# FFT filter and two gated layers on one core: the first batch's FFT kept on chip, float64 weights joined in two VectorE steps, order of instructions left to the scheduler

## The chip, the core and the metric

The kernel runs on one core of a Trainium2 chip. The metric is the time of one execution in device microseconds (us). Five engines work side by side, each through its own queue in order: TensorE (PE, matmuls; its weight loads are listed as PEld), VectorE (DVE), ScalarE (ACT), GpSimd (POOL) and SyncE (SP, which here only issues transfers). ACT and POOL issue transfers too. A transfer runs on 16 DMA engines that all queues share. TensorE writes only to PSUM; DVE and ACT bring results from there to SBUF; POOL works in SBUF alone.

## The reference

```python
def _attn_ref(x, filt_r, filt_i):            # x: 8 x 3072 x 256
    X = np.fft.rfft(x, axis=1)
    Y = X * (filt_r + 1j * filt_i)[None]
    return np.fft.irfft(Y, n=x.shape[1], axis=1).astype(np.float32)

def _moe_ref(x, w_in, w_out, g_ln):          # per token: 256 -> 1024 -> 256
    h = x @ w_in
    e = np.exp(h - np.max(h, axis=-1, keepdims=True))
    solu = h * (e / (np.sum(e, axis=-1, keepdims=True) + 1e-09))
    mu, var = mean(solu), mean((solu - mu) ** 2)
    return ((solu - mu) / np.sqrt(var + 1e-06) * g_ln) @ w_out

def _moe2_ref(x, w1, w2, w3, w_out):         # 256 -> 768 -> 256
    return np.maximum(np.maximum(x @ w1, x @ w2), x @ w3) @ w_out
```

x and the filter are float32; the six weight matrices are float64.

## The kernel before

There are 8 batches of 3072 rows and 256 columns. Each batch goes through four FFT steps: a (a transform over 128 points), b (over 24 points, with the filter's products), c (24 points back) and d (128 points back). Behind d come the layers, in six tiles of 512 tokens for each batch: h (x @ w_in, four pieces of 128 tokens), z (@ w_out), m (the three maxout products, six pieces), o (the last product, two pairs). That makes 48 tiles; the main loop runs over them and, for each, through a string of tokens (`ORDER`, for the first tile `FIRST`), which names the pieces in the order in which they are written. FFT steps of the next batches lie between them (`slots`, s0 to s4). Batches 1 to 7 run in float16 pairs (high and low parts), three matmuls for one product.

Batch 0 comes first and alone: its four FFT steps run in float32 ahead of the main loop. `first_a` (L282) computes step a and writes it to DRAM (`scr_a0`). For each of eight groups u, `first_load_b` reads a piece of it back in another layout, `first_b` (L294) does step b, `products` (L229) the filter, `first_turn` (L310) turns the result with TensorE transposes, and `first_c` (L325) does step c and writes to DRAM (`scr_0`), from which `load_d` reads the tiles of step d. The tables of steps b and c come as 144 KB pieces for each u.

Between these steps the weights are prepared (`steps`, `fills`, `jobs`). A block of float64 is loaded as pairs of 32-bit words (`wload`), turned to float32 in `wprep` (ACT takes the high word as a float, L615, and POOL raises small values, L616) and `wconv` (three VectorE steps on integers, L628, L630, L632), 20 blocks in all. `colsum` (ACT, PE, DVE) bounds the size of each matrix, `wscale` makes a power of two of it, and `wsplit` (L669 to L676) writes the float16 pairs. `center_wo1` takes the column mean off w_out.

The whole program stands in `tc.manual_schedule()`: each engine gets its instructions in the order in which the code writes them. The `run` helper delays the late half of an item behind the next item's matmuls.

Of the kernel before, what the change touches and what calls it, by code (L numbers as in the profile page):

```python
# [9 lines left out]
I32 = mybir.dt.int32  # L10
BF16 = mybir.dt.bfloat16
# [16 lines left out]
def kernel(  # L28
# [47 lines left out]
    scr_a0 = drm.tile([128, 24, 256], F32, name="scr_a0")  # L76
# [6 lines left out]
    b_f, c_f = (  # L83
        t[:, 1].rearrange("p k h s -> p (k h s)").bitcast(F32).rearrange("p (u q s) -> u p q s", u=8, q=4)
        for t in (dft_b, dft_c)
    )
    dft_b, dft_c = dft_b[:, 0], dft_c[:, 0]
# [114 lines left out]
    spare = []  # L202

    def first_load_b(u):
        t = two.tile([96, 4, 256], F32, tag="bin", name="bin0")
        src = scr_a0.rearrange("k n d -> (k n) d").rearrange("(u q p) d -> u p q d", q=4, p=96)
        SP.dma_start(out=t, in_=src[u])
        bin_t[0, u] = t
# [6 lines left out]
    def first_load_c(u):  # L215
        if u % 2 == 0:
            t = two.tile([96, 768], F16, tag="ct", name="ct0", bufs=1)
        else:
            t = spare[0][:96]
        t = t.bitcast(F32).rearrange("p (q s) -> p q s", q=4)  # L220
        SP.dma_start(out=t, in_=c_f[u])
        ct_t[0, u] = t
# [6 lines left out]
    def products(pss, ft, u):  # L229
        yfs = []  # L230
        for dc in range(2):
# [10 lines left out]
            G.tensor_tensor(p1[:, :, 0, :], p1[:, :, 0, :], p2[:, :, 1, :], op=ALU.subtract)  # L242
            G.tensor_tensor(p1[:, :, 1, :], p1[:, :, 1, :], p2[:, :, 0, :], op=ALU.add)
            if u == 0:
                G.tensor_copy(p1[:, 0, :, 0], t)
            yfs.append(p1)
# [35 lines left out]
    def first_a(s):  # L282
        pss = []
        for h in range(2):
            ps = rtile("aps")
            c = s * 1024 + h * 512
            PE.matmul(ps, dA_f, x_t[0][:, c:c + 512], start=True, stop=True)
            pss.append(ps)
        ao = two.tile([128, 1024], F32, tag="ao" if s % 4 < 2 else "yt", name="ao0")
        S.activation(ao[:, 0:512], pss[0], AF.Copy)  # L290
        V.tensor_copy(ao[:, 512:1024], pss[1])
        SP.dma_start(out=scr_a0[:, 4 * s:4 * s + 4, :], in_=ao.rearrange("p (n d) -> p n d", n=4))

    def first_b(u):  # L294
# [11 lines left out]
        def out():  # L306
            yT_t[0, u] = products(pss, f_t.pop((0, u)), u)
# [16 lines left out]
    def first_c(u):  # L324
        yt, ct = yT_t.pop((0, u)), ct_t.pop((0, u))  # L325
        zf = two.tile([128, 1024], F32, tag="ao", name="zf")
        pss = []
        for i in range(2):
            ps = rtile("cps")
            for q in range(2):  # L330
                c = (2 * i + q) * 256
# [864 lines left out]
```

## Time and profile before

| | us |
|---|---|
| median of 3 runs | 2925.84 (2925.73 to 2934.33) |
| profiled execution, its own time | 2924.07 |
| its span, first to last instruction | 2922.3 |
| TensorE busy / idle in the span | 2804.4 / 117.9 |
| VectorE busy | 1987.1 |
| ScalarE busy | 1203.8 |
| GpSimd busy | 1154.4 |
| mean granted TensorE clock | 0.985 of 2.4 GHz |

The profile is one execution. Its span is 1.8 us shorter than its own time, and that is 1.8 us under the median. A busy TensorE is counted from modelled ends of pipelined matmuls, so "busy" there means that work is in its queue without a gap. The rows that matter come below.

### The profile page before, as it was taken

How to read it: one execution, taken by the hardware profiler on the slowest of the kernel's cores; microseconds unless marked ns; L12 is line 12 of the kernel's file. 1: busy time of each engine (PE TensorE's matmuls, PEld its weight loads, DVE VectorE, ACT ScalarE, POOL GpSimd, SP SyncE). 2: the span in 40 equal slices, each digit the busy share in tenths (PEclk: the TensorE clock that was granted, in tenths of full speed). 3: DMA queues.
4: the chain of work that ended last, by engine and by line, in shares of the span. 5: the costliest groups of instructions: out<-in, count | busy, mean ns of one | idle time of the engine just before them, and what ended most of it. 6: DMA issues, size and time to landing. Idle time of an engine off the chain costs nothing. (4 is left out here: it accounts for less than half of the span.)

```text
span 2922.3 us, 48692 instructions
## 1 busy us (share of the span) xinstructions
PE 2804.4 (96%) x18676; PEld 1545.9 (53%) x18676; DVE 1987.1 (68%) x3932; ACT 1203.8 (41%) x1988; POOL 1154.4 (40%) x1205
## 2 busy tenths in 40 slices
PE   6689999999999999999999999999999999999999
PEld 4444554455545555555555555555555555555555
DVE  6787676676767677767766777667677667656553
ACT  3454444343444344434444443444344443433332
POOL 4542562444334443344433443344433444333322
PEclk7899999999999999999999999999999999999999
DMA  8433795476545764458534774447654466322221
GB/s 293 128 98 94 181 201 110 124 152 135 119 111 124 144 157 98 115 126 175 125 93 120 147 171 90 136 112 150 142 121 110 102 145 144 82 63 60 55 62 29
DMA packets 726504, 361.07 MB, mean 124 GB/s; under 512 B 620992, under 2 KB 672064, under 8 KB 726272
## 3 DMA queue, kind: packets, MB, share of 16 engines
q1 hardware_dynamic: 697168, 250.96, 38.8%
q0 software_dynamic: 28960, 106.95, 13.8%
q8 instruction: 146, 2.39, 0.4%
q14 instruction: 86, 0.70, 0.1%
q10 hardware_dynamic: 144, 0.07, 0.0%
HBM read 130.32 MB, written 75.50 MB: 70 GB/s over the span
## 5 line engine op out<-in xcount | busy, mean ns | idle before, releaser
L483 POOL TENSOR_TENSOR ul<-u,uh 128x1024 f16<-128x1024 f32 x191 | 406.3, 2127 | 1085.5 <-issue 625.4
L542 PE MATMUL mps<-z,wm 128*128 128x512 f16 x1728 | 655.0, 379 | 25.0 <-DVE am L550 16.8
L543 PE MATMUL mps<-z,wm 128*128 128x512 f16 x1728 | 655.0, 379 | 0.0
L544 PE MATMUL mps<-z,wm 128*128 128x512 f16 x1728 | 654.8, 379 | 0.0
L550 DVE SCALAR_TENSOR_TENSOR am<-mps,am 128x512 f32<-128x512 f32 x576 | 396.7, 689 | 231.0 <-ACT am L548 162.2
L452 ACT ACTIVATE u<-hps,mx,scl 128x1024 f32<-128x1024 f32 (+1 forms) x195 | 232.2, 1191 | 417.7 <-DVE mx L449 410.8
L446 DVE TENSOR_REDUCE mx<-hps 128x1 f32<-128x1024 f32 (+1 forms) x195 | 234.4, 1203 | 204.7 <-PE hps L437 204.0
L554 POOL TENSOR_TENSOR h<-am,h 128x512 f16<-128x512 f32 x240 | 279.4, 1164 | 212.5 <-ACT h L553 212.3
L482 ACT ACTIVATE uh<-u 128x1024 f16<-128x1024 f32 x192 | 202.9, 1057 | 322.5 <-DVE u L463 322.4
L553 ACT ACTIVATE h<-am 128x512 f16<-128x512 f32 x288 | 181.3, 629 | 369.9 <-DVE am L550 369.9
L463 DVE SCALAR_TENSOR_TENSOR u<-hps,mx,u 128x1024 f32<-128x1024 f32 (+1 forms) x195 | 246.8, 1267 | 106.4 <-ACT u L452 89.2
L569 PE MATMUL ops<-wo,h 128*128 128x256 f16 x1152 | 314.7, 273 | 4.5 <-ACT o L575 4.5
L570 PE MATMUL ops<-wo,h 128*128 128x256 f16 x1152 | 314.8, 273 | 0.0
L571 PE MATMUL ops<-wo,h 128*128 128x256 f16 x1152 | 314.8, 273 | 0.0
L435 PE MATMUL hps<-win,y 128*128 128x512 f16 x768 | 293.3, 382 | 6.7 <-DVE u L463 6.7
L437 PE MATMUL hps<-win,y 128*128 128x512 f16 x768 | 293.6, 382 | 0.2 <-DVE y L411 0.2
L436 PE MATMUL hps<-win,y 128*128 128x512 f16 x768 | 293.4, 382 | 0.0
L543 PEld LDWEIGHTS <-wm 128*128 128x128 f16 x1728 | 169.1, 98 | 230.6 <-issue 38.6
L522 PE MATMUL zps<-ln,wo 128*128 128x512 f16 x752 | 287.1, 382 | 2.4 <-ACT o L575 2.4
L523 PE MATMUL zps<-ln,wo 128*128 128x512 f16 x752 | 287.1, 382 | 0.0
L544 PEld LDWEIGHTS <-wm 128*128 128x128 f16 x1728 | 169.1, 98 | 204.0 <-issue 0.3
L542 PEld LDWEIGHTS <-wm 128*128 128x128 f16 x1728 | 169.2, 98 | 198.7 <-ACT wst L671 0.3
(207 smaller groups left out, 4344.7 us busy)
## 6 DMA issues: line engine op xcount, KB each, us to landing
scr_a<-ao SPq DMA_DIRECT2D x48, 512.0 KB, 3.5
out_dram<-o SPq DMA_DIRECT2D x95, 256.0 KB, 2.3
xt<-in_x_dram POOLq DMA_DIRECT2D x42, 512.0 KB, 5.9
ft<-in_filt_dram POOLq DMA_DIRECT2D x56, 384.0 KB, 5.3
bin<-scr_a POOLq DMA_DIRECT2D x56, 384.0 KB, 5.2
scr_z<-zt SPq DMA_DIRECT2D x56, 384.0 KB, 3.6
din<-scr_z POOLq DMA_DIRECT2D x42, 512.0 KB, 5.3
bt<-in_dft_b_dram POOLq DMA_DIRECT2D x56, 144.0 KB, 4.1
```

The source lines that it names most:

```text
L435: PE.matmul(o, y[:, dc, 0, tk], win[:, 0, dc, w], start=(dc == 0), stop=False)
L436: PE.matmul(o, y[:, dc, 0, tk], win[:, 1, dc, w], start=False, stop=False)
L437: PE.matmul(o, y[:, dc, 1, tk], win[:, 0, dc, w], start=False, stop=(dc == 1))
L483: (V if (b, g, i) == (0, 0, 3) else G).tensor_tensor(ul, u, uh, op=ALU.subtract)
L522: PE.matmul(ps, wo1[:, 0, c, w], ln[:, 0, c], start=(c == 0), stop=False)
L542: PE.matmul(pss[k], wm[k][:, 0, dc, w], z[:, dc, 0], start=(dc == 0), stop=False)
L543: PE.matmul(pss[k], wm[k][:, 1, dc, w], z[:, dc, 0], start=False, stop=False)
L544: PE.matmul(pss[k], wm[k][:, 0, dc, w], z[:, dc, 1], start=False, stop=(dc == 1))
L550: V.scalar_tensor_tensor(am, ps, 2.0 ** -15, am, op0=ALU.mult, op1=ALU.max)
L569: PE.matmul(o, h2[:, j, 0, tk], wo2[:, 0, j], start=(j == 0), stop=False)
L570: PE.matmul(o, h2[:, j, 0, tk], wo2[:, 1, j], start=False, stop=False)
L571: PE.matmul(o, h2[:, j, 1, tk], wo2[:, 0, j], start=False, stop=(j == 5))
```

## The change

**On chip.** `scr_a0` and its round trip go. `first_a` now takes x as the stationary operand (48 matmuls of 128 columns in place of 12 of 512), so that its result stands with d on the partitions, and writes it to two SBUF tiles. `first_turn_a` turns each group with eight TensorE transposes and two ACT copies. `first_c` swaps its operands as well, its result goes to an SBUF tile `zx`, and `first_turn_z` turns it (eight transposes for each of six tiles). Only tiles 2 to 5 of step d still go through DRAM.

**Tables and filter.** Both float32 tables of a group u come in one transfer, all eight issued at the start, into the space of the later weights (`wm`, `wo2`). The filter is loaded into `win`, `wo1` and others. The filter's scale goes into step d (`ky`).

**Weights.** `wprep` computes a float32 on ACT with a factor, and POOL makes from the 16 bits in the middle of each float64 the low word that rounds right; `wconv` then needs two VectorE steps, both with two tensor inputs. w_out is prepared first, w_in next, w1 and w2 next in the second `ln` buffer, w3 in `yt` buffers, w_out2 last.

**Order.** `tc.manual_schedule()` goes, and the scheduler sets each engine's order. In the first tile h0 and h1 of the second tile move from ahead of the loop to `FIRST`.

On PE one round of batch 0's FFT was, before (eye_f is the identity, yps a transposed product, cps step c, bps step b):

```order
L332 MATMUL cps<-yt_429,ct_372 96x256 x4
L300 MATMUL bps<-bt_416,bin_418 128x96 x8
L316 MATMUL yps<-eye_f,p_516 96x128 x4
L316 MATMUL yps<-eye_f,p_522 96x128 x4
L332 MATMUL cps<-yt_505,f_115 96x256 x4
```

and is now, with the turning of step a (tps) in it:

```order
L336 MATMUL cps<-wm_77,yt_387 128x96 x8
L301 MATMUL bps<-wm_79,bi 128x96 x8
L321 MATMUL yps<-eye_f,yhl_90 96x128 x4
L321 MATMUL yps<-eye_f,yhl_91 96x128 x4
L287 MATMUL tps<-eye_f,a_104 96x128 x8
L336 MATMUL cps<-wm_78,yt_456 128x96 x8
```

A round grew by eight transposes, and step c is cut as step b is.

On ACT, around the first use of batch 0's step d (y is its float16 pair, which h needs; wab is the colsum's input), before:

```order
L321 ACTIVATE yt_726<-yps 96x1024
L337 ACTIVATE zf<-cps,pf 96x512 x2
L644 ACTIVATE wab<-wo_193 128x1024
L644 ACTIVATE wab<-wo_194 128x1024
L615 ACTIVATE wst<-wln 128x2x256 x2
L337 ACTIVATE zf<-cps,pf 96x512 x2
L675 ACTIVATE wo_76<-wo_193,pwo_791 128x1024
L675 ACTIVATE wo_76<-wo_194,pwo_791 128x1024
L410 ACTIVATE y<-dps,scl 128x512 x2
```

and now (zx is step c's result on chip, zps its transposes, din the input of step d):

```order
L341 ACTIVATE zx<-cps 128x24x16 x2
L707 ACTIVATE win<-win_125,pwin 128x1024
L707 ACTIVATE win<-win_126,pwin 128x1024
L362 ACTIVATE din_860<-zps_855 128x512
L643 ACTIVATE w_880<-wln 128x512
L643 ACTIVATE w_881<-wraw 128x256
L740 ACTIVATE wmean<-wmean 128x256
L676 ACTIVATE wab<-wo_123 128x1024
L676 ACTIVATE wab<-wo_124 128x1024
L362 ACTIVATE din_909<-zps_899 128x512
L436 ACTIVATE y<-dps,ky 128x512 x2
```

The split of w_out (wo_76) left the stretch ahead of y; its column mean (wmean) and the sizes behind it (wab) stand ahead of y now as then.

On DVE, in a late tile without FFT work, where h's second piece meets the first m pieces (u is h's product, am the maximum of the three m products, BN the statistics of u), before:

```order
L459 TENSOR_SCALAR mx<-st,scl 128x1
L463 SCALAR_TENSOR_TENSOR u<-hps,mx,u 128x1024
L550 SCALAR_TENSOR_TENSOR am<-mps,am 128x512 x6
L446 TENSOR_REDUCE mx<-hps 128x1
L449 TENSOR_SCALAR mx<-mx,scl 128x1
L467 BN_STATS mv<-u 128x6 x2
```

and now:

```order
L485 TENSOR_SCALAR mx<-st,scl 128x1
L489 SCALAR_TENSOR_TENSOR u<-hps,mx,u 128x1024
L576 SCALAR_TENSOR_TENSOR am<-mps,am 128x512
L493 BN_STATS mv<-u 128x6
L576 SCALAR_TENSOR_TENSOR am<-mps,am 128x512
L493 BN_STATS mv<-u 128x6
L494 BN_AGGR mv<-mv 128x2
L576 SCALAR_TENSOR_TENSOR am<-mps,am 128x512
L495 COPY st<-mv 128x1
L576 SCALAR_TENSOR_TENSOR am<-mps,am 128x512 x3
```

The statistics moved from behind the next piece's maximum, where ACT's exponential left DVE free, to between the am steps. On PE the sequence of pieces is the same from the second batch's step b on, to the end. POOL's queue now begins with five transfers of batch 1 (two table pieces, two filter pieces, one table c) and, behind the last matmul of `first_a`, the reload of dA.

The diff, cut:

```diff
+REBIAS = 2.0 ** -112
+TOP = (1 - 2.0 ** -8) * 2.0 ** -13
-FIRST = "s0 s1 h2 m0 x0 x1 m1 x0 m2 s2 x0 x0 x0 x0 x2 h3 m3 d m4 m5 g0 f o0 s3 o2 g1 s4"
+FIRST = "h0 m0 x0 h1 m1 x0 x0 h2 m2 x0 x0 x0 s0 s1 s2 x2 h3 m3 d m4 m5 g0 f o0 s3 o2 g1 s4"
...
+    bc_f = dft_b[:, 1:3].rearrange("p t k h s -> p (t k h s)").bitcast(F32).rearrange("p (u q s) -> u p q s", u=8, q=8)
...
     def first_load_tab(u):
-        t = two.tile([96, 4, 96], F32, tag="bt", name="bt0")
-        SP.dma_start(out=t, in_=b_f[u])
-        bt_t[0, u] = t
+        w = (wm + [wo2])[u // 2]
+        names = "h c n" if u < 6 else "h j n"
+        t = w[:96, u % 2].rearrange(f"p {names[2:]} -> p ({names[2:]})").bitcast(F32).rearrange("p (q s) -> p q s", q=8)
+        SP.dma_start(out=t, in_=bc_f[u])
+        bt_t[0, u], ct_t[0, u] = t[:, 0:4], t[:, 4:8]
...
     def first_a(s):
+        for dc in range(2):
+            ps = rtile("aps")
+            for n in range(4):
+                c = s * 1024 + n * 256 + dc * 128
+                PE.matmul(ps[:, n * 128:(n + 1) * 128], x_t[0][:, c:c + 128], dA_f, start=True, stop=True)
+            pv = ps.rearrange("p (n i m) -> p i m n", n=4, i=2)
+            S.activation(af[0][:, dc, :, 4 * s:4 * s + 4], pv[:, 0], AF.Copy)
+            V.tensor_copy(af[1][:, dc, :, 4 * s:4 * s + 4], pv[:, 1])
+
+    def first_turn_a(u):
+        av = af[u // 4].rearrange("p e (q m) n -> p e q (m n)", q=16)
+        bi = two.tile([128, 1024], F32, tag="ao", name="bi")
+        bin_t[0, u] = bi[:96].rearrange("p (q d) -> p q d", q=4)
         pss = []
-        for h in range(2):
-            ps = rtile("aps")
-            c = s * 1024 + h * 512
-            PE.matmul(ps, dA_f, x_t[0][:, c:c + 512], start=True, stop=True)
+        for i in range(2):
+            ps = rtile("tps")
+            for q in range(2):
+                for dc in range(2):
+                    c = q * 256 + dc * 128
+                    PE.transpose(ps[:96, c:c + 128], av[:, dc, 4 * (u % 4) + 2 * i + q], eye_f)
             pss.append(ps)
-        SP.dma_start(out=scr_a0[:, 4 * s:4 * s + 4, :], in_=ao.rearrange("p (n d) -> p n d", n=4))
+
+        def out():
+            for i in range(2):
+                S.activation(bi[:96, i * 512:i * 512 + 512], pss[i][:96], AF.Copy)
+        return out
...
     def first_c(u):
-                PE.matmul(ps[:96, q * 256:q * 256 + 256], ct[:, 2 * i + q], yt[:96, c:c + 256], start=True, stop=True)
+                PE.matmul(ps[:, q * 96:(q + 1) * 96], yt[:96, c:c + 128], ct[:, q], start=True, stop=True)
...
+                S.activation(
+                    zx[0][:, :, dc, 16 * u:16 * u + 16],
+                    pss[dc][:, :384].rearrange("p (m n) -> p n m", n=24), AF.Copy,
+                )
...
+    def first_turn_z(g):
...
+                    PE.transpose(ps[:, c:c + 128], zx[0][:, 4 * g + 2 * i + n, dc], eye_f)
...
+        if g < 2:
+            din_t[0, g] = t
+        else:
+            SP.dma_start(out=scr_0[:, 4 * g:4 * g + 4, :], in_=t)
...
-            S.activation(dst, raw.bitcast(F32).rearrange("p a (n w) -> p a n w", w=2)[:, :, :, 1], AF.Abs)
-            G.tensor_scalar(dst, dst, LEAST, None, op0=ALU.max)
+            S.activation(dst, raw.bitcast(F32).rearrange("p a (n w) -> p a n w", w=2)[:, :, :, 1], AF.Copy, scale=REBIAS)
+            lo = raw.rearrange("p a (n w) -> p a n w", w=2)[:, :, :, 0]
+            top = raw.bitcast(U16).rearrange("p a (n w) -> p a n w", w=4)[:, :, :, 1]
+            G.tensor_scalar(lo, top, TOP, 7.5 * 2.0 ** -8 - 0.5, op0=ALU.mult, op1=ALU.add)
...
-            V.tensor_scalar(bits, bits, 3, 0x3FFFFFF8, op0=ALU.logical_shift_left, op1=ALU.bitwise_and)
+            V.scalar_tensor_tensor(lo, hi, -0x80000000, lo, op0=ALU.bitwise_and, op1=ALU.bitwise_or)
         for bits, lo, hi in wide:
-            V.scalar_tensor_tensor(bits, hi, -0x40000000, bits, op0=ALU.bitwise_and, op1=ALU.bitwise_or)
-        for bits, lo, hi in wide:
-            V.scalar_tensor_tensor(bits, lo, 29, bits, op0=ALU.logical_shift_right, op1=ALU.bitwise_or)
+            V.scalar_tensor_tensor(bits, bits, 3, lo, op0=ALU.logical_shift_left, op1=ALU.bitwise_or)
...
-    with tc.manual_schedule():
...
+    for i in range(11):
+        b_out = first_b(i - 1) if 0 < i < 9 else None
+        t_out = first_turn(i - 2) if 1 < i < 10 else None
+        a_out = first_turn_a(i) if i < 8 else None
...
+        c_out = first_c(i - 3) if i > 2 else None
...
+    first_turn_z(0)
+    cen[4]()
```

## Rows read from the trace of the kernel before

**Rows 1.** Busy time of each engine over the whole span, from the page.

```profile
PE 2804.4 (96%) x18676; PEld 1545.9 (53%) x18676; DVE 1987.1 (68%) x3932; ACT 1203.8 (41%) x1988; POOL 1154.4 (40%) x1205
```

**Rows 2.** Windows: stretch, PE, PEld, DVE, ACT, POOL busy us, TensorE clock, DMA share, GB/s.

```profile
15.00:20.00 5.00, 2.69 (x7) 0.90 (x5) 5.00 (x7) 1.19 (x2) 0.00 (x0) 1.00 1.03 420
```

**Rows 3.** Windows of the FFT, of the tile behind it, and of a late one.

```profile
50.00:100.00 50.00, 39.94 (x223) 32.19 (x223) 37.47 (x69) 27.96 (x42) 34.80 (x41) 0.89 0.61 179
100.00:150.00 50.00, 28.02 (x177) 16.79 (x176) 39.22 (x88) 23.35 (x36) 19.26 (x13) 0.76 0.34 106
...
2750.00:2800.00 50.00, 50.00 (x287) 26.88 (x285) 30.12 (x62) 18.29 (x31) 14.62 (x10) 1.00 0.26 59
```

**Rows 4.** TensorE's waits, 0 to 260 us: who for whom, us, times, longest.

```profile
PE bps L300 <- issue: 15.2, 1, 15.2
PE wps L652 <- ACT wab L644: 13.0, 5, 4.4
PE dps L396 <- DMA din<-scr: 8.6, 1, 8.6
PE yps L316 <- POOL p L243: 7.5, 7, 2.1
PE hps L435 <- DVE u L463: 6.7, 1, 6.7
```

**Rows 5.** TensorE's waits, 260 us to the end, the first and the third.

```profile
PE mps L542 <- DVE am L550: 14.9, 18, 1.1
...
PE ops L569 <- ACT o L575: 4.5, 3, 2.1
```

**Rows 6.** TensorE's timeline, start and us: batch 0's steps, the first h, the second tile's z.

```profile
4.90 12.79 PE L287 MATMUL aps<-xt,dA 128*128 128x512 f32 x24 [4.90 <-DMA xt<-in_x_dram]
32.89 7.11 PE L300 MATMUL bps<-bt,bin 96*128 96x96 f32 x32 [15.21 <-issue]
...
45.46 3.57 PE L300 MATMUL bps<-bt,bin 96*128 96x96 f32 x16
...
85.95 1.92 PE L300 MATMUL bps<-bt,bin 96*128 96x96 f32 x16
...
111.46 3.75 PE L396 MATMUL dps<-dD,din 128*128 128x128 f32 x16 [8.58 <-DMA din<-scr]
115.00 0.50 PE L435 MATMUL hps<-win,y 128*128 128x512 f16 x1
...
221.45 0.38 PE L522 MATMUL zps<-ln,wo 128*128 128x512 f16 x1
```

**Rows 7.** TensorE's timeline: transposes at either clock, the column mean, a later step d.

```profile
42.57 1.09 PE L316 MATMUL yps<-eye_f,p 128*96 128x128 f32 x4 [2.57 <-POOL p L245]
...
79.89 1.04 PE L316 MATMUL yps<-eye_f,p 128*96 128x128 f32 x8
...
82.50 3.62 PE L704 MATMUL wmean<-wo,ones 128*128 128x256 f32 x16
...
149.96 2.05 PE L396 MATMUL dps<-dD,din 128*128 128x128 f32 x16 [0.31 <-DVE u L463]
```

**Rows 8.** Groups of 0 to 221 us on DVE, POOL and ACT: count, busy, mean ns.

```profile
L616 POOL TENSOR_SCALAR wst<-wst 128x512 f32<-128x512 f32 x12 | 19.5, 1635 | 22.8 <-ACT wst L615 22.8
...
L242 POOL TENSOR_TENSOR p<-p,p 128x192 f32<-128x192 f32 x16 | 11.4, 710 | 7.7 <-DVE p L236 7.7
...
L337 ACT ACTIVATE zf<-cps,pf 96x512 f32<-96x512 f32 x16 | 10.5, 677 | 2.7 <-PE cps L332 2.4
...
L628 DVE TENSOR_SCALAR wst<-wst 128x512 int32<-128x512 int32 x12 | 9.6, 824 | 6.7 <-POOL wst L616 6.7
...
L321 ACT ACTIVATE yt<-yps 96x1024 f32<-96x1024 f32 x8 | 8.1, 1015 | 18.0 <-PE yps L316 18.0
...
L711 POOL TENSOR_TENSOR wo<-wo,wmean 128x256 f32<-128x256 f32 x8 | 6.6, 861 | 0.0
...
L630 DVE SCALAR_TENSOR_TENSOR wst<-wln,wst 128x512 int32<-128x512 int32 x6 | 5.7, 972 | 0.0
```

More of the change, by code (lines that the diff above doesn't have):

```diff
@@ L10 @@
 I32 = mybir.dt.int32
+U16 = mybir.dt.uint16
 BF16 = mybir.dt.bfloat16
@@ new lines @@
+    src = x[0].rearrange("(p r) d -> p (r d)", r=24)
+    x_t[0] = one.tile([128, 6144], F32, tag="x", name="xt")
+    for i in range(6):
+        SP.dma_start(out=x_t[0][:, i * 1024:(i + 1) * 1024], in_=src[:, i * 1024:(i + 1) * 1024])
+    S.dma_start(out=dA_f, in_=dft_a[:, 2:4].rearrange(flat).bitcast(F32))
+    G.dma_start(out=eye_sb, in_=eye)
+    load_filter()
+    V.memset(ones, 1.0)
+    V.memset(mhalf, -0.5)
+    V.memset(alpha_w, 1.0)
+    V.tensor_copy(eye_f, eye_sb)
+    ut = [two.tile([128, 1024], F32, tag="bin", name="wo32") for _ in range(2)]
@@ new lines @@
+    yt = [two.tile([128, 2, 2, 512], F16, tag="y", name="win32") for _ in range(2)]
+    wo1_32 = [wview(t, 4, 256) for t in ut]
+    win_32 = [wview(t.rearrange("p a b c -> p (a b c)").bitcast(F32), 1, 1024) for t in yt]
+    todo = [b for i in range(2) for b in blocks(w_out, wo1_32[i], 4 * i)]
+    todo += [(w_in[k * 128:(k + 1) * 128, c:c + 512], win_32[k][:, :, c:c + 512])
+             for k in range(2) for c in (0, 512)]
+    wm_32 = [wview(wln[1].bitcast(F32)[:, k * 1536:], 2, 768) for k in range(2)]
@@ new lines, in pre, with job, conv @@
+    def pre(i):
+        def job():
+            wprep(todo[i][1], got[i])
+        return job
+    def conv(*n):
+        return lambda: wconv([(todo[i][1], got.pop(i)) for i in n])
+    first_load_tab(0)
+    load_f(0)
+    for u in range(1, 8):
+        first_load_tab(u)
+        load_f(u)
+        if u < 6:
+            get(u - 1)()
+    G.dma_start(out=dD_f, in_=dft_d[:, 2:4].rearrange(flat).bitcast(F32))
+    G.dma_start(out=gsb, in_=g_ln.rearrange("(c p) -> p c", p=128))
+    for s in range(6):
+        first_a(s)
+        absmax(0, s)
@@ new lines, in split, with scale, job, pads @@
+    def split(dst, v, nm, eng=V):
+        return lambda: wsplit(dst, v, pw[nm], eng)
+    def scale(nm, c0, n):
+        def job():
+            pw[nm] = wscale(wmax[:, c0:], n, nm)
+        return job
+    def pads():
+        for t in yhl_t:
+            G.memset(t[:, :, 96:128], 0.0)
+    zx.append(one.tile([128, 6144], F32, tag="x", name="zx").rearrange("p (n e m) -> p n e m", n=24, e=2))
+    cso = colsum(wo1_32, 256, wmax, 2)
+    csw = colsum([v[:, :, :] for v in win_32], 1024, wmax, 0)
@@ new lines @@
+    h(0)
+    cso[0]()
+    for i in range(17, 19):
+        get(i)()
+    h(1)
+    cso[1]()
+    scale("o1", 2, 1)()
+    split(wo1[:, :, 0:4], wo1_32[0], "o1")()
+    split(wo1[:, :, 4:8], wo1_32[1], "o1")()
+    first_turn_z(2)
+    h(2)
+    pre(16)()
+    conv(16)()
+    for f in cs[0]:
+        f()
+    first_turn_z(3)
+    z_part(0)
+    cs[1][0]()
+    h(3)
+    cs[1][1]()
+    z_part(1)
+    for f in cs[2]:
+        f()
+    run(d_item(0, 1))
+    flush()
+    z_part(2)
+    scale("m", 4, 6)()
@@ new lines, in split_m @@
+    def split_m(k, c):
+        eng = (V, G, G)[k]
+        if k < 2:
+            split(wm[k][:, :, :, c:c + 384], wm_32[k][:, :, c:c + 384], "m", eng)()
+            return
+        for i in range(2):
+            split(wm[k][:, :, i:i + 1, c:c + 384], yts[i][:, :, c:c + 384], "m", eng)()
+    for k in (2, 1, 0):
+        split_m(k, 0)
+    z_part(3)
+    for k in (2, 1, 0):
+        split_m(k, 384)
+    first_turn_z(4)
+    first_turn_z(5)
+    get(19)()
+    wo2_32 = wview(one.tile([128, 6144], F32, tag="x", name="wst"), 6, 256)
```

475 lines of the change are left out of this document (210 added, 265 removed).

## The prediction

> **What bounds the kernel now.** I read the busy shares first. TensorE is busy 2804.4 us of a span of 2922.3 [rows 1], so 117.9 us are idle, and no other engine is above 68%. The windows show where the idle time lies: a late stretch of 50 us is busy for all 50 at the full clock of 2.4 GHz, while 50 to 100 us is busy 39.94 at a granted clock of 0.89 and 100 to 150 us only 28.02 at 0.76 [rows 3]. So the late tiles are bound by TensorE's own work, which the change leaves in number and order, and the start is bound by chains through other engines. TensorE's waits of the first 260 us name them: 15.2 us ahead of the first step b, 13.0 for the sizes of the weights, 8.6 for step d's input from DRAM, 7.5 for POOL's products, 6.7 for a DVE product [rows 4]. After 260 us the waits are many and small; the largest sum, 14.9 us, is in 18 pieces of 1.1 at most [rows 5].
>
> The timeline gives four marks: step a runs from 4.90 to 17.7, the first step b starts at 32.89, the first h at 115.00, and the second tile's z, from which on the order is nearly the same, at 221.45 [rows 6]. I sum the change between these marks, against the profiled execution's own 2924.07 us; the median of the runs lies 1.8 above it.
>
> **Step a to the first step b.** Now 12.79 us for step a, then 15.2 of waiting for the DRAM round trip [rows 4, 6]. After: 48 matmuls of 128x128 in float32. Eight of them (16 records) in step d took 2.05 us at full clock [rows 7], so 6 x 2.05 = 12.3 us, from 4.90 to 17.2. Then one copy out of PSUM, eight transposes and two more copies. The nearest copy is 0.677 [rows 8], eight transposes are 1.04 at full clock [rows 7]: 17.2 + 0.7 + 1.0 + 1.4 = 20.3. The five transfers of batch 1 that now stand at the head of POOL's queue are 1.23 MB; at the 420 GB/s that the engines moved in this stretch [rows 2] they can push the loads behind them back by 2.9 us, so 20.3 to 23.2. I take 22.5, near the upper end, since the first pass through each engine is included in it. Against 32.89 that is 10.4 us earlier. The removed writes and reads of `scr_a0` (6.3 MB) free more transfer time than the 1.23 MB take.
>
> **The eight rounds.** Now step b of the third group starts at 45.46 and that of the eighth at 85.95 [rows 6], 40.5 us for five rounds, 8.1 each. After, TensorE has in one round eight transposes of step a, eight matmuls of step b, eight transposes of the products and eight matmuls of step c, which now has step b's shape. At full clock 1.04 + 1.92 + 1.04 + 1.92 = 5.9 us; at half clock (3.57 for step b at 45.46, 1.09 for four transposes) 2.2 + 3.6 + 2.2 + 3.6 = 11.6 [rows 6, 7]. ACT: two new copies of 0.677, one of 1.015, two for step c at 0.677 at most [rows 8], so 3.7, and about 1.7 of weight work, 5.4. POOL: four product steps of 0.710 and 1.5 blocks of `wprep` at 1.635 [rows 8], 5.3. DVE was busy 37.47 of 50 there [rows 3], 6.1 of each 8.1; it loses a join step of 0.824 for each block [rows 8], 1.2 a round, and one of the two left writes with a stride. POOL's new form, with 16-bit strided input, is not in the trace: its floor is the old 1.635, and at twice that a round on POOL is 7.7. A round therefore costs between 5.9 (TensorE, all else hidden) and 8.1 (as now). I take 7.3, nearer to today's value, because the chain step b, DVE, POOL, transposes stays and is what TensorE waits for now, while the waits on loads go. The eighth step b then starts at 22.5 + 7 x 7.3 = 73.6.
>
> Here **a rule speaks against the change**. The trace shows the eight transposes at 79.89 in 1.04 us, 0.13 each, and step b six microseconds later at its fast 1.92 [rows 6, 7]: transposes did not keep the clock down there. The Trainium skill, "TensorE: Matmul & The Clock Gate", section "Part 4: PE-mode transpose", says that the full clock does not engage for a transpose and gives about 275 ns for one in a real kernel. By that the 112 added transposes would cost 31 us instead of 112 x 0.13 = 14.6, and more of the PE's rounds would run at half rate; the row decides for the smaller figure, and what the slower clock would give stands among the rivals.
>
> **From the last step b to the first h.** Step b 1.9, products on DVE and POOL about 4, transposes 1.0, copy 1.0, step c 1.9, two copies 1.4, transposes of `zx` 1.0: 73.6 + 12.2 = 85.8. No DRAM lies between; the 8.6 us of waiting [rows 4] is gone. But what is late next is the order on ACT: the pair y that h needs stands behind the column mean and both sizes (wab). The mean takes 3.62 on TensorE [rows 7], to 89.4; its copy 0.4; POOL takes it off in 8 steps of 0.861 [rows 8], 6.9, to 96.7; then one size, one copy and the first y, each near 0.7 to 1.0. h starts at about 99. Step d's own 2.05 is hidden beside POOL's 6.9. Against 115.00 that is 16 us earlier.
>
> **From h to the second tile's z.** Now 106.4 us, DVE busy 39.22 of the first 50 [rows 3]. Added: four turns of `zx` on TensorE (4.2 to 8.8), eight ACT copies at 0.677 (5.4), the scale and split of w_out, which were finished ahead of h before. Taken away: a join step in eight blocks on DVE, 8 x 0.824 = 6.6 if the two left cost no more than before (0.972 [rows 8]), and the 6.7 us [rows 4] in front of an h piece, since both h pieces of the second tile now lie between m pieces that TensorE can do meanwhile. Bounds: 8 us better (DVE's saving in full and part of the wait) to 10 worse (all turns and copies on the path). I take 0, as the added work is on the engines that have room and the removed on the one that is near its limit. The gain at 221.45 is 16 us.
>
> **The 47 tiles behind.** TensorE's sequence is the same. What moved is the order on DVE, ACT and POOL. On DVE the statistics of u now lie between the am steps. In a late tile that costs nothing: two pieces of m hold six PSUM buffers, so DVE is only late when it falls a whole m piece behind. In tiles with FFT work it can cost. On ACT the store's first copy now comes ahead of uh, which helps the waits on it (4.5 us at one line [rows 5]). Gain and loss have no row; the nearest are the waits that exist, 14.9 and 4.5 us, so at most some 20 us better, and, with one more wait of 0.8 (14.9 / 18) in each of some 36 tiles with FFT work, 29 worse. I take 0, the row of today.
>
> The sum: 2924.07 - 16 = 2908 for a profiled execution, **2910 us** for the median.
>
> **Rivals.** (1) The clock stays at 1.2 GHz through the rounds. For it: step b at 45.46 still took 3.57, against 1.92 at 85.95 [rows 6], and a round has more short transposes than now. Against: 0.89 on the mean from 50 to 100 us and the fast rows there [rows 3, 6]. A round is then 11.6 us on TensorE; the point from which the change loses is 7.3 + 16 / 7 = 9.6 us a round. At 11.6 the first h is at 129 instead of 99, 14 later than now, and the time is 2924 + 14 + 2 = 2940. By the section of the Trainium skill named above this would be the likely case; the rows speak against it. (2) The gain of 16 us is eaten behind h: turns, copies and the split of w_out all lie on the path (10 us), and POOL's new form is slow (another 3 to 6 in the rounds): 2920 to 2926, no change that can be told. (3) The new order opens a wait in each FFT tile, DVE in statistics or a product while TensorE needs an am step: 36 x 0.8 = 29 us, 2910 + 29 = 2939. For it: DVE and POOL share the work of these tiles in an order set without this chip's waits. Against: the tiles have two m pieces of slack. (4) The new order removes waits: 2910 less 10 to 20, 2890 to 2900.
>
> **How the numbers follow.** Forecast and its bounds of 2896 to 2917: 0.52. Rival 4: 0.13. Rival 2: 0.18. Rival 1: 0.09. Rival 3: 0.08. Within 0.3% is 8.8 us, about what a measurement of this kernel can tell from no change: faster means below 2917.1, slower above 2934.6. Faster: 0.52 + 0.13 = 0.65. Same: rival 2 and the milder halves of 1 and 3, 0.18 + 0.02 = 0.20. Slower: 0.15. The range of eight in ten reaches from 2890, the end of rival 4, to 2937, which takes in rival 2 and part of 1 and 3.
>
> **What would show it.** In the profile after: first step b near 22.5, rounds of 7.3, the first h near 99 and waiting for y behind the sizes, the second tile's z near 205; TensorE's idle time behind that point near 40 us as now. A first h after 107 makes the rounds wrong (look at the granted clock and at POOL's `wprep`); an h near 99 with z after 212 makes the middle wrong; z near 205 and a time over 2917 means the new order in the tiles costs.

## The result, and the profile after

The kernel after the change takes 2903.35 us (2896.60 to 2906.97, median of 4 runs). Its ratio to the kernel before is 0.990 (95% interval 0.9878 to 0.9922), some 29 us less (the two medians of this group of runs, 2928.59 for the kernel before, lie 25 apart). 2910 was forecast, with a range of 2890 to 2937. The profiled execution took 2904.83 us, 19.2 less than that of before, and its span is 2903.1. From one group of runs to the next the median of the kernel before lay between 2926.6 and 2936.1, so the experiments are compared by their ratio to it.

The busy time of the engines, from the page of the kernel after (before: [rows 1]):

```profile
PE 2804.4 (97%) x18923; PEld 1561.0 (54%) x18924; DVE 2048.4 (71%) x3918; ACT 1236.9 (43%) x2024; POOL 1139.9 (39%) x1208
```

Over the whole span TensorE is busy exactly as long as before, so by the sums the whole gain is idle time. It is not the same work, though. Up to the second tile's z (line of before, then of after, columns as in the windows below):

```profile
0.00:221.45 221.45, 155.07 (x870) 102.08 (x871) 162.41 (x314) 97.39 (x143) 106.27 (x106) 0.84 0.55 172
```

```profile
0.00:193.68 193.68, 156.75 (x1118) 116.96 (x1119) 150.35 (x310) 109.93 (x183) 92.75 (x117) 0.94 0.61 166
```

TensorE has 248 records more there, 112 of them transposes, and is busy hardly longer, at a mean granted clock of 0.94 instead of 0.84. The idle time up to that z fell from 66.4 to 36.9 us. So the higher clock has a part in the gain of the start: it paid for the added work. DVE is busy 61 us longer over the whole span, although it has 18 instructions of the join less; that comes back below. The windows of the start (stretch, busy us of PE, PEld, DVE, ACT, POOL, then TensorE's granted clock, DMA share, GB/s; before: [rows 3]):

```profile
0.00:50.00 50.00, 40.88 (x327) 39.32 (x328) 34.74 (x62) 24.50 (x48) 22.97 (x46) 1.00 0.99 298
50.00:100.00 50.00, 37.18 (x252) 30.64 (x252) 39.00 (x84) 31.84 (x53) 26.59 (x36) 0.90 0.27 86
100.00:150.00 50.00, 40.47 (x340) 26.46 (x338) 42.80 (x96) 35.15 (x56) 22.54 (x17) 0.94 0.62 146
```

The granted clock is 1.00 of 2.4 GHz for the first 50 us, in which TensorE now runs without the pause of 15.2 us [rows 4]; before it was 0.73 there, and the two steps b behind the pause ran at half clock, 7.11 us for 32 records [rows 6]. And the stretch from 100 to 150 us holds 40.47 us of busy time instead of 28.02. TensorE's timeline, at the marks of [rows 6] (start, us, the work, in brackets the wait ahead of it):

```profile
21.58 2.02 PE L301 MATMUL bps<-wm,bi 96*128 96x96 f32 x16 [0.36 <-ACT bi L292]
...
42.10 1.95 PE L301 MATMUL bps<-wm,bi 96*128 96x96 f32 x16
...
44.76 1.04 PE L287 MATMUL tps<-eye_f,a 128*96 128x128 f32 x8
45.63 1.92 PE L336 MATMUL cps<-wm,yt 96*128 96x96 f32 x16
47.39 2.04 PE L301 MATMUL bps<-wm,bi 96*128 96x96 f32 x16
...
58.02 1.95 PE L301 MATMUL bps<-wo,bi 96*128 96x96 f32 x16
...
75.64 3.76 PE L738 MATMUL wmean<-wo,ones 128*128 128x256 f32 x16
...
89.41 0.61 PE L461 MATMUL hps<-win,y 128*128 128x512 f16 x1 [7.36 <-ACT y L436]
...
193.68 0.38 PE L548 MATMUL zps<-ln,wo 128*128 128x512 f16 x1
```

The first step b starts 11.3 us earlier than before, the eighth 27.9, the first h 25.6, the second tile's z 27.8. From that z to the end of the execution, though, the kernel after takes 2904.83 - 193.68 = 2711.2 us, and the kernel before took 2924.07 - 221.45 = 2702.6. So 8.5 us of the gain are given back in the tiles. TensorE's waits from 260 us on show where (who for whom, us in total, times, longest; before: [rows 5]):

```profile
PE mps L568 <- DVE y L433: 36.9, 26, 2.9
PE bps L242 <- DMA bin<-scr_a: 6.8, 1, 6.8
PE mps L568 <- ACT am L574: 5.6, 1, 5.6
```

The waits for am that led the list before, 14.9 us, are gone, and a wait that did not exist has come: m's matmuls wait 26 times for y, the low half of step d's result. They do not read y; they take the PSUM buffers of step d from the same ring, and those are free only when y is written. All waits behind 260 us sum to 57.8 us, 16.8 more than the 41.0 of before; a wait of 6.5 us between 221 and 260 us of before is gone. That leaves 10.3 for the 8.5 that the marks give.

### The profile page after: what moved, and what is told of

The parts are those of the page before. It is cut to its first block, busy times and chain, and to the rows that moved or that the text cites. A ratio compares the mean times of both kernels' runs of the same rounds, so it can differ in the third digit from the quotient of the medians.

```text
span 2903.1 us, 49134 instructions
## 1 busy us (share of the span) xinstructions
PE 2804.4 (97%) x18923; PEld 1561.0 (54%) x18924; DVE 2048.4 (71%) x3918; ACT 1236.9 (43%) x2024; POOL 1139.9 (39%) x1208
## 4 chain that ended last, share of the span: by engine, by line
PE 76%; DVE 11%; issue 4%; DMA 4%; POOL 3%; ACT 2%; SPq 0%; POOLq 0%; ACTq 0%; DVEq 0%
PE mps L568 10%; PE mps L570 9%; PE mps L569 9%; PE zps L548 5%; PE zps L551 5%; PE zps L549 5%; PE hps L461 5%; PE hps L462 5%; PE hps L463 5%; PE ops L596 4%; PE ops L597 4%; PE ops L595 4%; DVE st L497 2%; DVE am L576 2%; DVE mx L472 1%
## 5 line engine op out<-in xcount | busy, mean ns | idle before, releaser
L568 PE MATMUL mps<-z,wm 128*128 128x512 f16 x1728 | 657.1, 380 | 45.2 <-DVE y L433 36.9
```

Source lines behind the costliest of these rows:

```text
L568: PE.matmul(pss[k], wm[k][:, 0, dc, w], z[:, dc, 0], start=(dc == 0), stop=False)
```

## The experiments

Marks from each profiled execution (us from the start of its span; "behind" is the span's end less z):

| kernel | ratio to before (95%) | first b | eighth b | first h | z, second tile | behind |
|---|---|---|---|---|---|---|
| before | 1 | 32.9 | 86.0 | 115.0 | 221.5 | 2700.8 |
| after | 0.9900 (0.9878, 0.9922) | 21.6 | 58.0 | 89.4 | 193.7 | 2709.4 |
| x1, before + scheduler | 0.9964 (0.9944, 0.9984) | 34.4 | 93.3 | 122.9 | 216.6 | 2702.1 |
| x10, before + join | 0.9981 (0.9957, 1.0006) | 34.3 | 88.2 | 116.2 | 218.4 | 2710.6 |
| x12, before + both | 0.9949 (0.9933, 0.9966) | 35.1 | 90.4 | 122.2 | 213.7 | 2705.2 |
| x6, after with the old join | 0.9990 (0.9975, 1.0006) | 21.1 | 72.8 | 111.3 | 219.2 | 2708.9 |
| x7, after with step a through DRAM | 0.9974 (0.9960, 0.9988) | 50.4 | 93.4 | 115.7 | 223.9 | 2705.4 |
| x11, after, POOL waits for ACT | 0.9939 (0.9919, 0.9960) | 21.6 | 68.8 | 96.2 | 200.3 | 2713.1 |
| x2, after in manual order | 0.9953 (0.9934, 0.9973) | 20.1 | 55.5 | 76.2 | 210.1 | 2718.7 |
| x3, after, loop in manual order | 0.9934 (0.9911, 0.9957) | 20.2 | 54.8 | 91.9 | 200.0 | 2712.3 |
| x4, after, DVE's loop in manual order | 0.9878 (0.9849, 0.9907) | 22.3 | 58.0 | 94.5 | 198.7 | 2699.4 |
| x5, after, y ahead of wab | 0.9874 (0.9858, 0.9890) | 21.4 | 56.5 | 87.0 | 191.1 | 2702.6 |
| x8, x4 + x5 | 0.9866 (0.9845, 0.9887) | 21.8 | 63.4 | 90.5 | 191.6 | 2698.3 |
| x9, x5 + priority for y | 0.9759 (0.9720, 0.9799) | 21.8 | 62.7 | 91.3 | 196.1 | 2661.9 |

**The order alone (x1), and taken back in whole or in part (x2 to x4).** x1 is the kernel before without its manual order; x2 to x4 are the kernel after with it, around everything, around the main loop, and around the main loop for VectorE alone.

```diff
# x1
-    with tc.manual_schedule():
# x2: ahead of the first load; x3: ahead of "for t in range(NT)"
+    with tc.manual_schedule():
# x4: ahead of "for t in range(NT)"
+    with tc.manual_schedule(engines={mybir.EngineType.DVE}):
```

> The kernel before with only the manual order taken away, so that the scheduler sets each engine's order; nothing of the on-chip FFT or of the two-step join. Theory A (the gain of the change is its start on chip, the scheduler's order costs time in the tiles because DVE's y of step d stands behind the statistics): the second tile's z stays near 221 us, TensorE waits for DVE y some 37 us in all behind 260 us as after the change, and the time is 2934 to 2945. Rival B (the scheduler's order of the start is what gains): z near 200 and 2905 to 2915. Rival C (the order does nothing either way): z near 221, no waits for y, 2922 to 2930.

> The kernel after with the manual order put back around the whole program, each engine in the order of the code. Theory A: the waits for DVE y are gone, the idle time of TensorE behind 260 us is near 41 us as before the change, z of the second tile between 194 and 205 since the start is on chip, and the time is 2886 to 2905. Rival B (the scheduler makes the start): z at 215 or later and 2915 or more. Rival C (order does nothing): 2903, z at 194, and the same waits on another releaser.

> The kernel after with the manual order put back for the main loop alone, all engines; the start stays with the scheduler. Theory A: z of the second tile near 194 as after the change, the 36.9 us of waits for DVE y gone, 8 to 17 us off the 2903: 2886 to 2895, the fastest of all. Rival C (the order in the tiles does nothing): 2900 to 2907. Rival D (what the tiles lose comes from POOL's and SP's loads, not from the order of the work): waits move from y to am and the time stays over 2898.

> As x3, but the manual order in the main loop holds for VectorE alone; ACT, POOL and SP stay with the scheduler there. Theory A (DVE's order is the cause): as x3 within 4 us, 2886 to 2897, no waits for DVE y. Rival E (the order of ACT and POOL counts as much): waits for y gone but others in their place, 2898 to 2910; ACT's own order could make DVE wait in the code's order, and then it is over 2910.

x1 has the waits for y, with the change's on-chip part absent: they belong to the scheduler's order. TensorE's waits of x1 from 260 us on, and of x4:

```profile
PE mps L542 <- DVE y L407: 36.7, 27, 2.9
```

```profile
PE mps L568 <- DVE am L576: 22.8, 21, 2.0
```

Beyond that theory A's numbers held only in part. x1 got faster, not slower: its start is 4.9 us shorter and its time behind z only 1.3 longer, so the order also gives something. In x4 the waits for y are gone and the time behind z is 10 us shorter than after, but am's waits are back, and its z came 5 us late, so the time does not stand apart from that of after: rival E's case at its edge rather than A's. The 5 us are not the edit's: the eighth step b is where it was, and from there to the first transposes of zx it takes 20.9 us instead of 15.9, with the granted clock at 0.50 from 70 to 80 us where after has 0.83. x2 and x3 miss A's numbers too. The 2921 us of x2 are what rival B asked for (2915 or more), though its z at 210.1 is not (215 or later). x3 is nearer to rival D. With ScalarE, POOL and SP in the code's order as well, step c of the next batches waits for its transposed input (waits of x2, then of x3):

```profile
PE cps L377 <- DMA yt<-yhl: 25.4, 5, 9.6
PE mps L568 <- DVE am L576: 17.2, 23, 1.1
```

```profile
PE cps L377 <- DMA yt<-yhl: 18.2, 4, 9.7
PE mps L568 <- DVE am L576: 17.6, 23, 1.1
```

In x2 the first h starts at 76.2, 13 us before that of after, and nothing remains of it at z: the matmuls of the sizes then wait 36.2 us for wab, in five pieces. So the code's order is good up to h and bad behind it, the scheduler's the other way round. Rival B, that the scheduler makes the start, falls by x1, rival C, that the order does nothing, by the waits of all four.

**The join taken back (x6), alone (x10), with the scheduler (x12); the DRAM round trip put back (x7).**

```diff
# x6 (x10 and x12: the reverse in the kernel before, x12 without its manual order)
-            S.activation(dst, raw.bitcast(F32).rearrange("p a (n w) -> p a n w", w=2)[:, :, :, 1], AF.Copy, scale=REBIAS)
...
-            G.tensor_scalar(lo, top, TOP, 7.5 * 2.0 ** -8 - 0.5, op0=ALU.mult, op1=ALU.add)
+            S.activation(dst, raw.bitcast(F32).rearrange("p a (n w) -> p a n w", w=2)[:, :, :, 1], AF.Abs)
+            G.tensor_scalar(dst, dst, LEAST, None, op0=ALU.max)
...
-            V.scalar_tensor_tensor(lo, hi, -0x80000000, lo, op0=ALU.bitwise_and, op1=ALU.bitwise_or)
+            V.tensor_scalar(bits, bits, 3, 0x3FFFFFF8, op0=ALU.logical_shift_left, op1=ALU.bitwise_and)
+        for bits, lo, hi in wide:
+            V.scalar_tensor_tensor(bits, hi, -0x40000000, bits, op0=ALU.bitwise_and, op1=ALU.bitwise_or)
         for bits, lo, hi in wide:
-            V.scalar_tensor_tensor(bits, bits, 3, lo, op0=ALU.logical_shift_left, op1=ALU.bitwise_or)
+            V.scalar_tensor_tensor(bits, lo, 29, bits, op0=ALU.logical_shift_right, op1=ALU.bitwise_or)
...
# x7
         first_a(s)
         absmax(0, s)
+    for u in range(8):
+        v = af[u // 4][:, :, 16 * (u % 4):16 * (u % 4) + 16]
+        SP.dma_start(out=scr_r[u], in_=v)
+        SP.dma_start(out=v, in_=scr_r[u])
```

> The kernel after with the weights joined as before: ACT takes the absolute high word, POOL raises small values (1.6 us a block instead of 0.79) and VectorE makes three steps of a block. Everything else as after. Theory H (POOL's and DVE's shorter steps are why a round of batch 0's FFT took 5.2 us where 7.3 was expected): rounds of 6.5 to 7.5, the eighth step b at 67 to 73 instead of 58.0, the first h at 95 to 105, z of the second tile at 200 to 206, and 7 to 13 us slower than the kernel after (ratio to before 0.992 to 0.995). Rival I (the rounds are TensorE's own 5.3 us of work, and POOL and DVE have room): rounds of 5.2 to 5.7, h at 89 to 92, within 4 us of the kernel after.

> The kernel after with a round trip through DRAM put back for step a: each of the eight groups of its result is written to DRAM and read back into its place ahead of its turning, 3.1 MB each way. Theory J (the on-chip start shifts everything behind it, since TensorE has no slack later): the first step b at 30 to 34 us instead of 21.6, the first h later by 5 to 12, z of the second tile at 199 to 206, and 5 to 12 us slower than the kernel after (ratio to before 0.992 to 0.995). Rival K (what comes before h is limited by the loads and the joining of the weights and by the wait for y, so that the round trip is hidden): first step b at 30 to 34, but h within 3 us of 89.4 and the time within 3 us of the kernel after.

> The kernel before with the two-step join of the weights alone (ACT takes the high word with its factor, POOL makes the low word, two VectorE steps); manual order, DRAM round trips and staging as before. x6 lost about 25 us against the kernel after when the old join was put back. Theory L (the join is worth that by itself, at any place): second tile's z at 196 to 206 instead of 221.5, 2900 to 2912 (ratio to before 0.990 to 0.993). Rival M (in the kernel before, the round trips through DRAM set the start, 15.2 and 8.6 us of waits, and the join only pays once they are gone): both waits as before, z at 212 to 221, 2914 to 2926 (ratio 0.995 to 1.000).

> The kernel before with the two-step join and with the scheduler's order, so that of the change only the on-chip FFT (and the staging that goes with it) is missing. The scheduler alone gave a ratio of 0.9964 and z of the second tile at 216.6, the join alone 0.9981 and 218.4. Theory R (the parts only pay together: while the DRAM round trips of 16 and 10 us stand, the start cannot get shorter by what is behind them): both round trips as long as before, z at 210 to 217, ratio to before 0.994 to 0.999. Rival S (join and scheduler make the change's gain between them, and the on-chip part is hidden): z at 195 to 203, ratio 0.988 to 0.992.

x6 shows theory H's mechanism at about twice its price. The rounds take (72.84 - 21.06) / 7 = 7.4 us, but h comes at 111 and the whole gain is gone. More than half of the 25.5 us by which z is late is the same TensorE work at a lower clock: up to z it is busy 170.68 us instead of 156.75, at 0.85 instead of 0.94.

```profile
0.00:219.24 219.24, 170.68 (x1117) 129.09 (x1119) 162.83 (x331) 111.73 (x183) 107.69 (x117) 0.85 0.52 146
```

The clock fell to half for the first time behind a wait of 4.55 us for POOL's product, ahead of the fourth step b. x10 shows rival M: alone in the kernel before the join gains nothing that can be told, with the round trips as they were. x12 adds the scheduler and still keeps both round trips (TensorE's waits up to 260 us of x12):

```profile
PE bps L303 <- DVE wraw L633: 17.0, 1, 17.0
PE dps L399 <- DMA din<-scr: 10.5, 1, 10.5
```

The first names a VectorE step, but the wait is the load's: the read of bin issued at 28.52 lands 6.5 us later, at 35.0, and step b starts at 35.14. The z of x12 at 213.7 is theory R's. x7 overshot: its eight reads stand behind the loads of tables and weights, and TensorE waits 28.7 us for them ahead of the first transposes, not the 9 to 12 that were meant, so it does not price the round trip of before. What it tells is that nothing hides such a wait: the first step b is 28.8 us later than after, z of the second tile 30.2, the span's end 26.2. Here too the clock has a part, since the first two steps b behind the wait ran at half rate (3.73 us each). So the parts do not all add. The order alone gives 0.4%, the join alone 0.2%, and the two 0.5%, about their sum; on-chip FFT with the order but without the join gives 0.1% (the intervals of x10 and x6 take in no change), and the three together 1.0%.

**What in the join made the rounds short (x11).** One more dependency: POOL must wait for ScalarE in each block. POOL's duration is kept; ScalarE gets a copy of 0.2 us a block more.

```diff
+            S.activation(raw.bitcast(U16).rearrange("p a (n w) -> p a n w", w=4)[:, :, 0:1, 0], dst[:, :, 0:1], AF.Copy)
             G.tensor_scalar(lo, top, TOP, 7.5 * 2.0 ** -8 - 0.5, op0=ALU.mult, op1=ALU.add)
```

> The kernel after with one more dependency in each of its weight blocks: POOL's low word has to wait for ScalarE's copy of the high word (a copy of one element by ScalarE into bytes that POOL overwrites), as POOL waited for it in the join of before. The durations on POOL and VectorE stay those of after. Theory P (the rounds got short because POOL no longer waits for ScalarE, and its products no longer stand behind such a wait): rounds of 6.3 to 7.4 as in x6, the eighth step b at 66 to 73, 10 to 25 us slower than the kernel after (ratio to before 0.993 to 0.999). Rival Q (they got short because POOL's step takes 0.79 us and not 1.56, and VectorE has a step less): rounds of 5.2 to 5.7, within 5 us of the kernel after.

POOL's largest group of the join from 20 to 115 us in x11, and one of x6 (count, busy, mean ns, idle time ahead and its releaser):

```profile
L647 POOL TENSOR_SCALAR wraw<-wraw 128x512 int32<-128x512 uint16 x10 | 7.4, 744 | 14.2 <-ACT wraw L646 8.3 <-issue 5.6
```

```profile
L646 POOL TENSOR_SCALAR wln<-wln 128x512 f32<-128x512 f32 x6 | 9.3, 1560 | 4.7 <-ACT wln L645 4.7
```

The duration stayed at 0.744, and a round went from 5.2 to (68.78 - 21.59) / 7 = 6.7 us, in the range of theory P and out of that of rival Q. But the price does not belong to POOL's wait alone. TensorE's timeline of x11:

```profile
35.50 1.08 PE L336 MATMUL cps<-wm,yt 96*128 96x96 f32 x4 [3.14 <-ACT yt L326]
...
41.19 3.62 PE L301 MATMUL bps<-wm,bi 96*128 96x96 f32 x16
...
50.38 1.95 PE L301 MATMUL bps<-wm,bi 96*128 96x96 f32 x16
```

The scheduler set the order anew. On ScalarE the first copy of turned products (yt) now stands behind a block's copy of the high word, which itself waits 1.45 us for its load; in after it came ahead of that copy. Behind this wait of 3.14 us the clock fell: from 35 to 50 us the granted clock is 0.54, and the round from 41.19 to 50.38 takes 9.19 us instead of 5.30 without a wait in it. Up to z TensorE is busy 162.77 us instead of 156.75 with the same matmuls and idle only 0.6 us longer: 6.0 of the 6.7 us by which z is late are the clock. And x8 and x9 below, whose start has the join of after, had such a stretch too (0.55 and 0.66 from 35 to 45 us, a wait of 1.16 and 1.47 us for POOL's product ahead of it); the line of x8:

```profile
38.51 3.62 PE L301 MATMUL bps<-wm,bi 96*128 96x96 f32 x16
```

Their rounds took 5.9 and 5.8 us. So of the 2.2 us a round between after and x6, the added dependency brings back 1.5 against after and 0.8 to 0.9 against x8 and x9, partly through ScalarE's order and the clock. That POOL's freedom from ScalarE is the larger part is therefore likely and not shown; what POOL's and DVE's shorter steps are worth by themselves was not run. At the end 0.4% of the 0.9% come back, and the interval of x11 touches that of after.

**The wait for y ahead of the first h (x5, x8).** y_ins holds the two ScalarE steps of the first y; x8 has x4's edit too.

```diff
-    cso[0]()
+    with tc.issue_after(y_ins[1].ins):
+        cso[0]()
```

> The kernel after with one constraint on ScalarE's order: the two sizes wab of w_out are issued behind the first pair y of step d, not ahead of it. In the profile of after, TensorE waits 7.4 us for that y, whose ACT queue stands behind POOL's 8 steps of 0.948 us on the column mean. Theory F (that wait is on the path that sets the end): the first h starts at 82 to 83 instead of 89.4, z of the second tile near 187 instead of 193.7, and the time falls by 5 to 8 us against the kernel after (ratio to before 0.987 to 0.988). Rival G (the split of w_out, now a little later, sets z_parts): h at 82, but z_parts wait longer for wo and z of the second tile stays at 192 to 195; no change in time (ratio 0.989 to 0.991).

> The edit of x5 together with that of x4 (VectorE in the order of the code in the main loop). By theory A and F the two gains add: no waits for DVE y behind 260 us, the first h 5 to 7 us earlier than in x4, 2890 to 2895 where x4 had 2899.5 (ratio to before 0.985). By rival G it is x4's time within 3 us.

The profiled x5 had its first transposes of zx at 77.7 us, where after has 73.9, and so h moved less than expected. Its eighth step b was 1.6 us early; behind it the granted clock was 0.50 from 60 to 80 us, where after has 1.00 and 0.83. From these transposes to h it is 9.3 us instead of 15.5, and from h to z 104.1 as against 104.3: h comes 6 us earlier than its inputs would have allowed before, and what follows moves with it, which is theory F. The times agree with it (0.9874) but do not prove it: the intervals of x5 and after overlap. In x8, from the transposes (79.5) to h is 11.0 against x4's 15.6; in time it is not told from x4, and it has 20.2 us of waits for am, so the two gains do not add as was expected.

**y ahead of the statistics (x9).**

```diff
-                    S.activation(y[:, dc, 0], pss[dc], AF.Copy)
-                    V.tensor_tensor(y[:, dc, 1], pss[dc], y[:, dc, 0], op=ALU.subtract)
+                    with tc.high_priority(offset=400):
+                        S.activation(y[:, dc, 0], pss[dc], AF.Copy)
+                        V.tensor_tensor(y[:, dc, 1], pss[dc], y[:, dc, 0], op=ALU.subtract)
```

> x5 (w_out's sizes behind the first y on ScalarE) with a higher priority for both steps of y, on ScalarE and VectorE, in all later batches; the scheduler still sets the order of everything else, so the statistics stay between the am steps. y then stands behind the two BN steps alone and ahead of the later statistics. Theory N (the waits for DVE y are y's place in VectorE's queue, and the statistics between the am steps cost nothing by themselves): the 37 us of waits for y fall below 12, no new waits over 8 for am, 2872 to 2888 where x5 had 2898 (ratio to before 0.980 to 0.984). Rival O (VectorE is simply late in these tiles, so that the wait moves to am or to another matmul): the sum of TensorE's waits behind 260 us stays within 10 us of x5's 53, and the time within 6 us of x5.

This is the fastest kernel: 2858.7 us (2857.33 to 2862.90), ratio 0.9759 (0.972 to 0.980), by the ratios 34 us under x5 ((0.9874 - 0.9759) x 2926.6), more than theory N's largest. VectorE's timeline in a tile of after:

```profile
614.39 1.28 DVE L493 BATCH_NORM_STATS2 mv<-u 128x6 f32<-128x512 f32 x2
615.59 1.61 DVE L497 SCALAR_TENSOR_TENSOR st<-st 128x4 f32<-128x4 f32 x1
617.12 0.20 DVE L494 BATCH_NORM_AGGREGATE mv<-mv 128x2 f32<-128x12 f32 x1
617.24 1.07 DVE L498 TENSOR_TENSOR st<-st 128x4 f32<-128x4 f32 x1
618.23 0.14 DVE L495 COPY st<-mv 128x1 f32<-128x1 f32 x1
618.29 1.27 DVE L433 TENSOR_TENSOR y<-dps,y 128x512 f16<-128x512 f32 x2
```

and in the same place of x9:

```profile
610.99 1.28 DVE L496 BATCH_NORM_STATS2 mv<-u 128x6 f32<-128x512 f32 x2
612.18 1.27 DVE L436 TENSOR_TENSOR y<-dps,y 128x512 f16<-128x512 f32 x2
613.37 0.20 DVE L497 BATCH_NORM_AGGREGATE mv<-mv 128x2 f32<-128x12 f32 x1
```

In after, y starts 3.90 us after the two BN steps began, in x9 1.19. TensorE's wait for y in that tile was

```profile
619.02 0.38 PE L568 MATMUL mps<-z,wm 128*128 128x512 f16 x1 [1.52 <-DVE y L433]
```

less than the 2.7 us that y moved. The waits of x9 from 260 us on begin with

```profile
PE bps L242 <- DMA bin<-scr_a: 7.1, 1, 7.1
PE cps L377 <- DMA yt<-yhl: 5.3, 2, 4.6
PE mps L571 <- DVE z L541: 2.6, 1, 2.6
```

and sum to 18.1 us instead of x5's 53.4; y has 0.8 left, and no matmul of m waits for am. Behind z, x9 is 40.7 us shorter than x5; 35.3 are these waits, and the other 5.4 are busy time of TensorE, 2639.9 us instead of 2645.3 for the same 17811 records, for which no cause was looked for.

## Why the prediction came out right

The time fell inside the range, and the sign and the likeliest case were right. But the sum was right because two errors cancelled. Against the forecast z at 205.45 and the 2908 of a profiled execution, z came 11.8 us early and the tiles cost 8.5: 2908.1 - 11.8 + 8.5 = 2904.8.

- **Step a to the first step b: right.** Forecast 22.5, measured 21.58. The five early transfers of batch 1 did not show.
- **The rounds: mis-sized.** Forecast 7.3 with bounds of 5.9 and 8.1, measured (58.02 - 21.58) / 7 = 5.2, below the lower bound. Three terms failed. The floor of 5.9 added durations of pipelined groups, which overlap: from the step b at 42.10 to that at 47.39 a full round is 5.29, eight transposes counting 0.87 and step c 1.76 from start to start. And POOL's step was given the old 1.635 as a floor, where the new form takes 0.788; the working did not see at all that the new form no longer waits for ScalarE (what that is worth lies between 0.8 and 1.5 us a round by x11, with the clock in it). And today's 8.1, near which the 7.3 was taken, holds stretches at half clock (0.85 on the mean from 50 to 86 us), where after has 1.00. With the old join (x6) a round takes 7.4, the value that was forecast, again with stretches at half clock. POOL's group up to 194 us in after:

```profile
L646 POOL TENSOR_SCALAR wraw<-wraw 128x512 int32<-128x512 uint16 x13 | 10.2, 788 | 16.3 <-DMA wraw<-in_w_out_dram 14.5 <-DVE st L484 1.1
```

- **From the last step b to h: the mechanism right, 6 us too short.** Forecast 25.4, measured 31.4. What follows the eighth step b, up to the column mean, took 17.6 instead of 12.2: step c of three groups, 1.76 us each, stands behind it on TensorE, where one was counted, and TensorE waits 2.7 us for products, which stand between weight blocks on POOL. From the mean to h it took 13.8, forecast 13.2, and what was named as late is what TensorE waits for: y, 7.36 us, behind POOL's steps on the mean, 7.31 in all, and the two wab.
- **From h to z: right.** Forecast no change of 106.4, measured 104.3.
- **The tiles: wrong.** Zero was taken, with "in a late tile that costs nothing". Of the am steps that is true, no matmul of m waits for them in x9 with the same interleaving. But y was not looked at, whose place on DVE decides when step d's PSUM is free. This is rival 3 in kind and size (28.8 us forecast as 36 x 0.8, measured 26 waits and 36.9 us) at another instruction, and it came together with the gain of rival 4, the 14.9 us for am.
- **The clock (rival 1) did not fall in the rounds of this execution, but it was near.** They ran at 1.00, and eight transposes took 1.04 us, as in [rows 7]. In x8 and x9, with the same instructions up to there, the fourth step b ran at half rate and the rounds took 0.6 to 0.7 us longer, so the 5.2 holds some luck. Behind the rounds the clock fell in after as well: 0.83 and 0.81 from 70 to 90 us, and behind the wait of 7.36 us for y the matmuls of h start every 0.43 us up to 92.8, every 0.22 from 93.1 on. The 275 ns a transpose of the Trainium skill ("TensorE: Matmul & The Clock Gate", section "Part 4: PE-mode transpose") does not hold for these float32 transposes: 0.87 us from start to start for eight is 0.11 each, at the full clock.
- **Rival 2** is refuted: nothing of the gain was eaten between h and z.

What stays open: how the gain of the rounds divides between POOL's wait, the shorter steps and the clock; why POOL's new form takes half the time of the old, and why step c waits for its transposed input in x2 and x3 more than in the kernel before; none of this was tried further.

## What to carry to other kernels

In a start that is a ring of engines, parts of a change do not add: undo one link and all of the gain may go, as the join did here, so price the ring and not the link, and ask of each step which engine it waits for before asking how long it takes. A wait can cost more than its length, since the matmuls behind it may run at half clock (up to z of x11, 0.6 us more idle time and 6.0 more of busy): read the granted clock of both runs before putting a difference down to the step that was edited. When a scheduler takes over an order that was written by hand, look for the instruction that frees a buffer for the bound engine, not only for the one that feeds it; a higher priority for the two steps of y was worth about as much here (34 us between x5 and x9) as the whole change (29).

## What the runs showed of the hardware

A VectorE step on 4 numbers a partition can take 1.9 us. The statistics st of the kernel before and of after, over the whole span (count, busy, mean ns):

```profile
L471 DVE SCALAR_TENSOR_TENSOR st<-st 128x4 f32<-128x4 f32 x48 | 7.3, 152 | 0.0
```

```profile
L497 DVE SCALAR_TENSOR_TENSOR st<-st 128x4 f32<-128x4 f32 x48 | 89.4, 1862 | 0.0
L498 DVE TENSOR_TENSOR st<-st 128x4 f32<-128x4 f32 x48 | 32.8, 684 | 0.0
```

It is the same instruction, and in x4, with DVE's order as before, it takes 152 ns again. POOL's timeline of after beside the tile above:

```profile
615.05 2.12 POOL L509 TENSOR_TENSOR ul<-u,uh 128x1024 f16<-128x1024 f32 x1 [1.89 <-ACT uh L508]
617.14 1.15 POOL L580 TENSOR_TENSOR h<-am,h 128x512 f16<-128x512 f32 x1
```

DVE's first st step starts at 615.59 inside POOL's ul and ends with it (617.20 and 617.17); its second starts inside POOL's h and ends with it (618.31 and 618.29). Both take two operands from SBUF. The Trainium skill, "SBUF — State Buffer", section "SBUF: two separate sides", says that such a step and a GpSimd step lock each other out for a whole instruction, whichever starts first; this trace agrees, with up to 3.45 us for one step; of the 48 first steps, 42 took over 0.3 us, and at least 28 of these end within 0.08 us of a GpSimd step that began before them. It is why y's place mattered so much: in this tile 2.68 of the 3.90 us ahead of y were these two steps.

The granted clock of TensorE fell to half behind waits, and the same matmuls then took almost twice as long: a float32 step b 3.62 us instead of 1.95, behind a wait of 4.55 us in x6, of 3.14 in x11, of 1.16 in x8.
